# One group's transpose of q moved from TensorE to the crossbar DMA, ahead of the next batch's loads

## Chip, cores, metric

The kernel runs on one core of one Trainium2 chip. The metric is the device time of one execution in microseconds (us), lower is better; medians of several runs are given. Times of day inside a run ("at 49.2") are us from the start of the span of the profiled execution, which is about 2 us shorter than the device time.

## The reference, cut to what matters

Eight batches of linear attention feed one gated feed-forward block. In the attention, q is normalised along the head dimension and k along the sequence:

```python
q_s = softmax over d of q          # batch 8, heads 8, seq 576, head_dim 64
k_s = softmax over s of k
kv  = einsum('bhsd,bhse->bhde', k_s, v)
x   = einsum('bhsd,bhde->bhse', q_s, kv)          # -> 4608 tokens x 512
out = (silu(x @ w_gate) * (x @ w_val)) @ w_out    # d_ff 1536
```

## The kernel before

A batch is done in two groups of four heads; "(1,0)" below is batch 1, group 0. For each group three loads bring q, k and v (576 KB each). ScalarE takes exp of q and k, VectorE sums and scales q (`norm`, giving the tile `qs`), and q must then be transposed, because x = q·kv contracts over d. The kernel has two ways to do it. `tr` uses nine TensorE transposes into PSUM (the accumulator memory, of which the kernel uses eight banks) and two VectorE copies; `tr_dma` uses one transposing DMA (called the crossbar transpose here) on SyncE's queue:

```python
def tr(b, G, piece, eng):                 # nine 128x128 transposes in two pieces
    tp = psp.tile([128, 1024], BF16, tag="ps", name="tp")
    for t in range(t0, t1):
        nc.tensor.transpose(out=tp[:, ...], in_=s["qs"][:, t, :], identity=ident)
    copy(eng, s["qta"][:, :, t0:t1, :], tp[...])
# ... cut ...
def tr_dma(b, G):
    qt = at.tile([128, T, 2, 64], BF16, tag="qtd", name="qtd")
    nc.sync.dma_start_transpose(out=qt..., in_=s["qs"]...)
```

`kv_kn` makes kv on TensorE and its scaled copy kn (half on ScalarE, half on VectorE with `split`). `x` multiplies kn and the transposed q into `xp` and copies it to `xt`, the input of the feed-forward block. `m_unit` is one of twelve units of gate and value products with Silu; `o_unit` is one block of 128 tokens of the output product, with its copy and its two stores. The argument is about the hand-over from batch 0 to the chunk of batch 1's last 448 tokens:

```python
load(1, 0, "q", q, after=w_dma[-3]); load(1, 1, "q", q)
for G in range(NG): load(1, G, "k", k); load(1, G, "v", v)
load_group(2, 0)                       # q, k, v of (2,0)
for m in range(MT): m_unit(0, S, m)
exp(1, 0, "q"); exp(1, 1, "q"); exp(1, 0, "k")
cast_v(1, 0, nc.gpsimd); cast_v(1, 1, nc.gpsimd)
load_group(2, 1)
o_unit(0, nc.scalar); norm(1, 0)
o_unit(1, nc.scalar); exp(1, 1, "k"); norm(1, 1)
o_unit(2, nc.scalar)
for piece in BANKS: tr(1, 0, piece, nc.vector)
kv_kn(1, 0, split=True)
for piece in BANKS: tr(1, 1, piece, nc.vector)
exp(2, 0, "q")
def between():                         # in the middle of o_unit(3)
    kv_kn(1, 1, split=True); x_both(1, 0, nc.vector)
finish = o_unit(3, between=between)
exp(2, 0, "k"); x_both(1, 1); finish()
norm(2, 0); tr_dma(2, 0)
cast_v(2, 0, nc.gpsimd); cast_v(2, 1, nc.gpsimd)
exp(2, 1, "q"); exp(2, 1, "k")
# ... then the chunk: m_unit 0, 1, 2, kv_kn(2,0), m_unit 3, 4, x_both(2,0) ...
```

Each engine, and each queue of DMA issues, executes its own part of this list strictly in this order.

The softmax here doesn't subtract the row's maximum and nothing guards it: scores larger than these inputs give would overflow.

## Time and profile before

| | before |
|---|---|
| device time, median of 3 | 319.42 us (319.02 to 320.06) |
| TensorE busy (profile page) | 310.4 of 317.4 us |
| TensorE at batch 0's last output block | starts 49.24 |
| fourth unit of the chunk starts | 59.31 |

The first line is from the profile's page, the busy time of the engines (PE is TensorE, PEld its weight loads, DVE VectorE, ACT ScalarE, POOL GpSimd).

```profile
PE 310.4 (98%) x1920; PEld 157.1 (50%) x1948; DVE 175.5 (55%) x332; ACT 149.2 (47%) x224; POOL 31.1 (10%) x33
```

TensorE is the bottleneck: nothing that delays it is made good later. Next, TensorE's own timeline in the hand-over. The columns are start, duration, engine, source line, operation, tiles and count; a bracket at the end gives idle time before the piece and what ended it.

```profile
47.29 0.67 PE L160 MATMUL tp<-ident,qs 128*128 128x128 bf16 x9
47.89 0.70 PE L184 MATMUL kv<-vb,ek 64*128 64x129 bf16 x18
48.73 0.68 PE L160 MATMUL tp<-ident,qs 128*128 128x128 bf16 x9
49.24 1.46 PE L297 MATMUL o_ps<-wo,hr 128*128 128x512 bf16 x5
...
53.55 1.41 PE L270 MATMUL g_ps<-xt,wg 128*128 128x448 bf16 x4
54.80 0.92 PE L270 MATMUL u_ps<-xt,wv 128*128 128x448 bf16 x4
...
59.31 0.93 PE L270 MATMUL g_ps<-xt,wg 128*128 128x448 bf16 x4
...
311.02 2.81 PE L318 MATMUL o_ps<-wo,hr 128*128 128x256 bf16 x36
```

The first line is the work that the change removes. The second set of transposes, group 1's, starts at 48.73. VectorE finishes their input at 48.68 (the next two lines, from VectorE's timeline, are the scaling of q of groups 0 and 1; 47.31 + 1.36 is 48.67), so they could not start earlier whatever TensorE did before.

```profile
44.35 1.36 DVE L140 TENSOR_TENSOR qs<-eq,rr 128x1152 bf16<-128x1152 bf16 x1
...
47.31 1.36 DVE L140 TENSOR_TENSOR qs<-eq,rr 128x1152 bf16<-128x1152 bf16 x1
```

ScalarE's timeline shows the exps of batch 2 (eq, ek), the half of kn that ScalarE makes, the xt copies, the table load and the first Silu of the chunk (sg). None has a bracket that names a DMA: the loads are there in time. They land at 49.0, 50.5, 52.0, 53.6, 55.1 and 56.5 (issue plus the time to landing of each load), 1.5 us apart.

```profile
50.17 1.16 ACT L115 ACTIVATE eq<-q 128x1152 bf16<-128x1152 f32 x1
51.58 0.63 ACT L206 ACTIVATE kn<-kv,kvr 64x64 bf16<-64x64 f32 x2 [0.24 <-DVE kvr L196]
52.23 1.16 ACT L115 ACTIVATE ek<-k 128x1152 bf16<-128x1152 f32 x1
53.42 0.70 ACT L104 CAST xt<-xp 128x320 bf16<-128x320 f32 x2
54.01 1.18 ACT L115 ACTIVATE eq<-q 128x1152 bf16<-128x1152 f32 x1
55.14 1.16 ACT L115 ACTIVATE ek<-k 128x1152 bf16<-128x1152 f32 x1
56.32 1.28 ACT L278 ACT_TABLE_LOAD   x1
57.62 1.42 ACT L278 ACTIVATE sg<-g_ps 128x448 bf16<-128x448 f32 x3
```

The table of stages gives, for each stretch of 2 us, the busy time of each engine, and at the end the granted TensorE clock (1.00 is full), the DMA engines' share and GB/s. Before the change the DMA is full throughout.

```profile
45.00:47.00 2.00, 2.00 (x11) 0.90 (x10) 1.98 (x2) 1.57 (x3) 1.72 (x1) 1.00 1.05 391
47.00:49.00 2.00, 1.86 (x35) 1.38 (x33) 1.95 (x4) 0.81 (x2) 1.31 (x1) 1.00 1.05 388
49.00:51.00 2.00, 1.95 (x26) 1.10 (x26) 1.90 (x8) 1.45 (x3) 0.68 (x1) 1.00 1.06 395
```

### The profile page before, as it was taken

The numbers are of one execution on the slowest core, as the hardware profiler recorded it, in microseconds if no ns is written. First come the engines' busy times: TensorE is split into PE (matmuls) and PEld (weight loads), VectorE is DVE, ScalarE is ACT, GpSimd is POOL, SyncE is SP. The second block draws the span as 40 slices with busy tenths as digits, with TensorE's granted clock in tenths as the row PEclk, the third lists the DMA queues.
The fourth block names the chain that finished last, engine by engine and source line by source line (L and its number), as shares of the span: only waits on it lengthen the run. The fifth ranks groups of instructions, "written<-read, shape, count | busy, mean of one in ns | idle before, by whom it ended". The sixth has DMA issues, their size and how long they took to land.

```text
span 317.4 us, 5037 instructions
## 1 busy us (share of the span) xinstructions
PE 310.4 (98%) x1920; PEld 157.1 (50%) x1948; DVE 175.5 (55%) x332; ACT 149.2 (47%) x224; POOL 31.1 (10%) x33
## 2 busy tenths in 40 slices
PE   8999999999999999999999999999999999999995
PEld 6777744554445444444444444444444444444444
DVE  2934479964647664774577366746575333333422
ACT  4753387744763475547364547355734122312300
POOL 1930023121100110011001100020000000000000
PEclk9999999999999999999999999999999999999999
DMA  7999999449145905392519440963150213020134
GB/s 269 252 190 206 281 392 393 130 116 367 22 84 153 379 24 103 74 385 94 103 38 355 162 103 1 310 241 64 41 103 2 44 22 67 3 61 5 35 67 99
DMA packets 39176, 46.34 MB, mean 146 GB/s; under 512 B 16368, under 2 KB 22384, under 8 KB 39152
## 3 DMA queue, kind: packets, MB, share of 16 engines
q1 hardware_dynamic: 33104, 41.17, 42.5%
q0 software_dynamic: 5808, 4.72, 9.7%
q8 instruction: 15, 0.25, 0.3%
q10 hardware_dynamic: 240, 0.13, 0.2%
q14 instruction: 9, 0.07, 0.1%
HBM read 37.75 MB, written 9.44 MB: 149 GB/s over the span
## 4 chain that ended last, share of the span: by engine, by line
PE 82%; DMA 10%; DVE 3%; POOL 2%; ACT 1%; issue 1%; SPq 0%; DVEq 0%; ACTq 0%
PE g_ps L270 26%; PE o_ps L297 26%; PE u_ps L270 26%; DMA wo<-in_moe_w_out_dram 5%; PE kv L184 2%; DMA v<-in_v_dram 2%; DMA q<-in_q_dram 2%; PE xp L218 1%; POOL wg L92 1%; POOL wv L92 1%; DVE qs L140 1%; PE o_ps L318 1%; DVE rs L131 1%; DVE xt L226 0%; SPq L77 0%
## 5 line engine op out<-in xcount | busy, mean ns | idle before, releaser
L278 ACT ACTIVATE sg<-g_ps 128x512 bf16<-128x512 f32 (+2 forms) x120 | 64.9, 554 | 132.9 <-PE g_ps L270 126.8
L279 DVE TENSOR_TENSOR hr<-sg,u_ps 128x512 bf16<-128x512 bf16 (+2 forms) x120 | 74.9, 633 | 90.7 <-PE u_ps L270 84.1
L270 PE MATMUL g_ps<-xt,wg 128*128 128x512 bf16 (+2 forms) x469 | 110.3, 358 | 0.7
L270 PE MATMUL u_ps<-xt,wv 128*128 128x512 bf16 (+2 forms) x468 | 109.6, 357 | 0.7
L297 PE MATMUL o_ps<-wo,hr 128*128 128x512 bf16 x415 | 93.3, 379 | 0.3
L270 PEld LDWEIGHTS <-wv 128*128 128x128 bf16 x480 | 46.9, 98 | 46.9 <-issue 0.3
L270 PEld LDWEIGHTS <-wg 128*128 128x128 bf16 x480 | 45.3, 98 | 46.2 <-issue 2.6
L297 PEld LDWEIGHTS <-hr 128*128 128x128 bf16 x420 | 41.0, 98 | 49.1 <-issue 0.2
L106 POOL CAST vb<-v 128x1152 bf16<-128x1152 f32 x14 | 17.8, 1270 | 167.2 <-DMA v<-in_v_dram 115.0
L131 DVE TENSOR_REDUCE rs<-eq 128x18 f32<-128x1152 bf16 x16 | 21.6, 1352 | 21.9 <-ACT eq L115 21.8
L106 DVE COPY o_sb<-o_ps 128x512 f32<-128x512 f32 x32 | 21.1, 686 | 20.6 <-PE o_ps L297 20.6
L140 DVE TENSOR_TENSOR qs<-eq,rr 128x1152 bf16<-128x1152 bf16 x14 | 19.8, 1415 | 0.5
L115 ACT ACTIVATE eq<-q 128x1152 bf16<-128x1152 f32 x16 | 18.5, 1163 | 3.2 <-DMA q<-in_q_dram 3.1
L115 ACT ACTIVATE ek<-k 128x1152 bf16<-128x1152 f32 x16 | 18.4, 1152 | 1.3 <-DMA k<-in_k_dram 1.3
L278 ACT ACT_TABLE_LOAD x12 | 15.4, 1283 | 0.2
L208 DVE TENSOR_SCALAR kn<-kv,kvr 64x64 bf16<-64x64 f32 x52 | 14.7, 283 | 1.3
L115 ACT ACT_TABLE_LOAD x11 | 14.1, 1283 | 0.9 <-DMA q<-in_q_dram 0.7
L104 ACT CAST xt<-xp 128x320 bf16<-128x320 f32 (+1 forms) x30 | 10.5, 402 | 6.6 <-PE xp L218 6.6
L226 DVE CAST xt<-xp 128x320 bf16<-128x320 f32 (+1 forms) x32 | 13.1, 450 | 0.5 <-PE xp L218 0.5
L249 PE MATMUL warm_ps<-zero 128*128 128x256 bf16 x80 | 10.9, 302 | 1.1 <-DVE zero L338 1.1
L184 PE MATMUL kv<-vb,ek 64*128 64x129 bf16 x288 | 10.3, 218 | 0.2 <-DVE vb L106 0.2
L184 PEld LDWEIGHTS <-ek 64*128 64x128 bf16 x288 | 8.4, 94 | 3.9 <-ACT sg L278 2.1
(32 smaller groups left out, 64.5 us busy)
## 6 DMA issues: line engine op xcount, KB each, us to landing
q<-in_q_dram SPq DMA_DIRECT2D x16, 576.0 KB, 7.0
k<-in_k_dram SPq DMA_DIRECT2D x16, 576.0 KB, 8.5
v<-in_v_dram SPq DMA_DIRECT2D x16, 576.0 KB, 9.4
out_dram<-o_sb SPq DMA_DIRECT2D x70, 128.0 KB, 2.4
wo<-in_moe_w_out_dram POOLq DMA_DIRECT2D x3, 512.0 KB, 19.0
wg<-in_moe_w_gate_dram POOLq DMA_DIRECT2D x2, 512.0 KB, 11.3
wv<-in_moe_w_val_dram POOLq DMA_DIRECT2D x2, 512.0 KB, 13.1
wg<-in_moe_w_gate_dram POOLq DMA_DIRECT2D x2, 256.0 KB, 6.0
```

The source lines that it names most:

```text
L106: eng.tensor_copy(out=out, in_=in_)
L115: nc.scalar.activation(out=s["e" + what], in_=raw[what, b, G].rearrange("p h (t d) -> p t h d", d=64), func=AF.Exp,)
L131: nc.vector.reduce_sum(out=rs, in_=s["eq"].rearrange("p t h d -> p (t h) d"), axis=mybir.AxisListType.X)
L140: eng.tensor_mul(s["qs"].rearrange("p t (h d) -> p (t h) d", d=64), s["eq"].rearrange("p t h d -> p (t h) d"), s["rr"].to_broadcast([128, ...
L184: nc.tensor.matmul(out=s["kv"][g][:, 0:129], lhsT=s["ek"][r, t, :, :].rearrange("p h d -> p (h d)"), rhs=s["vb"][r, t, 0:129], start=(t == 0),
L208: nc.vector.tensor_scalar_mul(out_, src, sc)
L226: nc.vector.tensor_copy(out=xt[:, 2 * G + 1, c0:c0 + n], in_=xp[1][:, 0:n])
L249: nc.tensor.matmul(out=ps[:, 0:256], lhsT=zero[:, 0:128], rhs=zero, start=True, stop=True)
L270: nc.tensor.matmul(out=p_[:, 0:w_], lhsT=w[:, kk, ms], rhs=xt[:, kk, c:c + w_], start=(kk == 0), stop=(kk == KT - 1),)
L278: nc.scalar.activation(out=sg[:, 0:w_], in_=g_ps[:, 0:w_], func=AF.Silu)
L279: nc.vector.tensor_mul(hr[:, m, r:r + w_], sg[:, 0:w_], u_ps[:, 0:w_])
L297: nc.tensor.matmul(out=o_ps, lhsT=hr[:, m, r0:r0 + 128], rhs=wo[:, m, :], start=(m == 0), stop=(m == MT - 1),)
```

## The change

The intent is to take nine transposes and two copies off TensorE and VectorE and let the DMA do them. The loads of batch 2 are moved behind the transpose in SyncE's order, so that the transpose does not have to queue behind 3.5 MB of loads.

```diff
@@ after batch 1's loads
             load(1, G, "v", v)
-        load_group(2, 0)
 
         for m in range(MT):
@@ hand-over
         cast_v(1, 1, nc.gpsimd)
-        load_group(2, 1)
         o_unit(0, nc.scalar)
         norm(1, 0)
+        tr_dma(1, 0)
+        load_group(2, 0)
+        load_group(2, 1)
         o_unit(1, nc.scalar)
         exp(1, 1, "k")
         norm(1, 1)
         o_unit(2, nc.scalar)
-        for piece in BANKS:
-            tr(1, 0, piece, nc.vector)
         kv_kn(1, 0, split=True)
```

## The prediction

> **What bounds the kernel.** TensorE: busy 310.4 of 317.4 us, clock granted in full (page). From 54.6 us on, the chain of waits is almost only TensorE, so a delay made by this change is paid to the end. The change lies in the hand-over from batch 0's products to the next chunk (39 to 60 us). There the DMA is full: 381 to 404 GB/s from 37 to 55 us (stage table).
>
> **Removed.** Nine transposes of (batch 1, group 0) on TensorE (0.68 us in the timeline, starting 47.3) and two VectorE copies of qt (0.82 us, 48.6). Neither is in the chain of waits: TensorE's next transposes, group 1's, start at 48.73 and wait for VectorE's qs of group 1, which ends at 48.68 whatever TensorE does. With group 0's gone, TensorE does kv at 47.4, then waits about 0.7 us for the same qs. Expected gain: 0 to 0.4 us.
>
> **Added.** One crossbar transpose on the SyncE queue. Other such transposes here take 1.3 us to issue and 3.2 us to land. It waits for qs of group 0 (45.7) and for the first output stores ahead of it on SyncE (about 45.2 to 46.4), so I put its issue at 46.4 and its landing at 49.7 to 50.5. Its reader, xp of group 0, runs at 51.3, so should not wait. (The Trainium skill, "Advanced Engine Details and Errata", X-Bar Transpose, says trn2 transposes are as fast as regular DMAs; here 295 KB (128x1152 bf16) take 3.2 us, while loads stream at about 390 GB/s; I use the trace.)
>
> **Moved.** All six loads of batch 2 (576 KB each, 1.5 us apart when streaming). Before, queued behind batch 1's, they land at 49.0, 50.5, 52.0, 53.6, 55.1, 56.5; the exps on ScalarE never wait. Afterwards they are issued only from 47.7, behind the transpose. The same sequence, transpose then six loads, stands twice in the trace (66.5 and 97.5): from the transpose's issue the loads land at about +5.5, +7.1, +8.9 to 9.8, +10.4 to 11.3, +12.3 to 12.8, +14. So q, k of group 0 land at about 51.9 and 53.5, q, k of group 1 at 57 and 58.9.
>
> **Critical path.** ScalarE runs in order: exp q (2,0), kn of group 1, exp k (2,0), xt copies, exp q, k (2,1), table load, first Silu. Late q pushes kn and xt: the chunk's start slips from 54.6 by about 1 us. Late k (2,1) puts the first Silu at 58.9 + 1.15 + 1.28 = 61.3 instead of 57.6. TensorE can run three units and kv ahead with eight banks; the fourth unit then needs the bank that the first Silu frees: 61.9 instead of 59.4. So about 2.5 us lost in all (not the sum), less a few tenths gained.
>
> **Prediction: 321.7 us**, 319.6 to 323.6 in 8 of 10. Faster by over 2%: 0.01; within 2%: 0.96; slower by over 2%: 0.03.
>
> **What shows it.** TensorE idles after kv of (1,0), group 1's transposes still start near 48.7; ScalarE shows waits for DMA q and k of batch 2 between 50 and 60 us (before: none); DMA rate dips at 45 to 49 us; first Silu of the second chunk at about 61 us; a TensorE wait for Silu near the fourth unit; from 65 us on the timelines run 2 to 3 us apart.
>
> **What would make it wrong.** Loads landing sooner after an earlier transpose issue (then 0 to 1 us lost, or slightly faster); xp waiting for a transpose that lands late (more lost); later transfers, shifted by 2 us, missing their readers.

## The result, and the profile after

The changed kernel takes 321.96 us (median of 6 runs, 321.31 to 322.98) against 319.35 us for the kernel before in the same rounds. The ratio is 1.0084 (95% interval 1.0061 to 1.0108), within 2%. Ratios are computed as the mean time of one kernel's runs over that of the other's of the same rounds, so they are not quite the ratio of the medians quoted. Executions over 1.5% slower than the fastest of the same kernel are left out of the means.

TensorE's timeline of the changed kernel, to be held against the one of before:

```profile
47.31 0.70 PE L184 MATMUL kv<-vb,ek 64*128 64x129 bf16 x18
48.30 0.68 PE L160 MATMUL tp<-ident,qs 128*128 128x128 bf16 x9 [0.29 <-DVE qs L140]
48.81 1.46 PE L297 MATMUL o_ps<-wo,hr 128*128 128x512 bf16 x6
50.20 0.70 PE L184 MATMUL kv<-vb,ek 64*128 64x129 bf16 x18
50.83 0.44 PE L218 MATMUL xp<-qtd,kn 64*64 64x320 bf16 x8
51.20 1.47 PE L297 MATMUL o_ps<-wo,hr 128*128 128x512 bf16 x6
52.60 0.32 PE L218 MATMUL xp<-qt,kn 64*64 64x320 bf16 x1
54.15 0.44 PE L218 MATMUL xp<-qt,kn 64*64 64x320 bf16 x7 [1.23 <-ACT kn L206]
54.52 0.55 PE L270 MATMUL g_ps<-xt,wg 128*128 128x448 bf16 x2
56.07 0.90 PE L270 MATMUL g_ps<-xt,wg 128*128 128x448 bf16 x2 [1.00 <-ACT xt L104]
...
62.46 0.93 PE L270 MATMUL g_ps<-xt,wg 128*128 128x448 bf16 x4
```

Group 0's transposes are gone and TensorE waits for qs of group 1 instead. VectorE finished it 0.43 us earlier in this trace (48.24), and the output block starts 0.43 us earlier, 48.81 against 49.24: the removal gained nothing there. xp of group 0 (50.83) reads the crossbar's result without a wait; the transpose was issued at 46.02 and landed 3.4 us later. Then come two waits that before did not have, 1.23 us for kn and 1.00 us for xt, both ScalarE's. SyncE's issues and ScalarE's timeline say why:

```profile
44.74 1.18 SPq L289 DMA_DIRECT2D out_dram<-o_sb  x2
46.02 1.41 SPq L172 DMA_TRANSPOSE qtd<-qs  x1
47.49 0.57 SPq L77 DMA_DIRECT2D q<-in_q_dram  x1
```

```profile
52.27 1.17 ACT L115 ACTIVATE eq<-q 128x1152 bf16<-128x1152 f32 x1 [3.29 <-DMA q<-in_q_dram]
53.46 0.64 ACT L206 ACTIVATE kn<-kv,kvr 64x64 bf16<-64x64 f32 x2
54.12 1.17 ACT L115 ACTIVATE ek<-k 128x1152 bf16<-128x1152 f32 x1
55.31 0.70 ACT L104 CAST xt<-xp 128x320 bf16<-128x320 f32 x2
56.69 1.17 ACT L115 ACTIVATE eq<-q 128x1152 bf16<-128x1152 f32 x1 [0.68 <-DMA q<-in_q_dram]
58.25 1.17 ACT L115 ACTIVATE ek<-k 128x1152 bf16<-128x1152 f32 x1 [0.39 <-DMA k<-in_k_dram]
59.43 1.28 ACT L278 ACT_TABLE_LOAD   x1
60.73 1.42 ACT L278 ACTIVATE sg<-g_ps 128x448 bf16<-128x448 f32 x3
```

ScalarE stands 3.29 us before exp of q (2,0), because that load was issued only at 47.49 and landed at 52.2. ScalarE takes its work in order, so kn and xt, which need nothing of batch 2, stand behind it. The loads of q, k of (2,0) and q, k of (2,1) land at 52.2, 53.6, 56.6 and 58.1 (issue plus time to landing; predicted 51.9, 53.5, 57 and 58.9), and the first Silu starts at 60.73 instead of 57.62. In the table of stages the DMA rate falls where before it was full (the run with the loads moved and no transpose has the same dip, 226, 184 and 373 GB/s, so the dip alone does not point to the transpose), and TensorE's clock falls a little later:

```profile
45.00:47.00 2.00, 2.00 (x12) 0.88 (x9) 1.93 (x4) 1.57 (x2) 1.29 (x1) 1.00 0.83 238
47.00:49.00 2.00, 1.71 (x30) 1.14 (x29) 1.93 (x5) 1.21 (x3) 1.61 (x1) 1.00 1.14 188
49.00:51.00 2.00, 2.00 (x32) 1.06 (x30) 0.90 (x4) 0.00 (x0) 0.24 (x1) 1.00 0.81 243
...
53.00:55.00 2.00, 0.85 (x9) 0.35 (x9) 0.84 (x4) 1.94 (x4) 0.00 (x0) 1.00 1.05 411
55.00:57.00 2.00, 1.00 (x4) 0.40 (x3) 1.97 (x4) 1.30 (x4) 1.15 (x1) 0.69 1.07 391
57.00:59.00 2.00, 2.00 (x6) 0.73 (x5) 1.93 (x3) 1.61 (x2) 0.00 (x0) 0.50 1.02 372
```

The granted clock of 0.50 near 57 to 59 was not in the prediction. It is there in two of the six runs by their mean clock (0.992 and 0.995, both 322.95 to 322.98 us); the four others have 1.000 and 321.31 to 322.12 us. The profile above is one of the two. The repeat below was profiled at full clock, and there the chunk's third and fourth matmul and its fourth unit read:

```profile
55.67 0.54 PE L270 MATMUL g_ps<-xt,wg 128*128 128x448 bf16 x2 [0.99 <-ACT xt L104]
56.04 0.92 PE L270 MATMUL u_ps<-xt,wv 128*128 128x448 bf16 x4
...
60.97 0.92 PE L270 MATMUL g_ps<-xt,wg 128*128 128x448 bf16 x4 [0.35 <-ACT sg L278]
...
312.67 2.81 PE L318 MATMUL o_ps<-wo,hr 128*128 128x256 bf16 x36
```

At full clock the fourth unit waits 0.35 us for the PSUM bank that the first Silu frees. At the halved clock TensorE was itself too slow to run into that wait: from the third matmul to the following kv it took 5.77 us (56.07 to 61.84) instead of 4.25 (55.67 to 59.92).

Not all of the loss lies in the hand-over. From the start of batch 0's output product (39.52 before, 39.59 in the repeat) to the last output block (311.02 and 312.67, the last lines of the two timelines) the repeat takes 1.6 us longer; I call this the long stretch below. From there to the end of the span it takes 6.80 us where before it is 6.35. This 0.4 us at the very end stands in every kernel here that has one more DMA than before (6.78 to 6.80 us; 6.72 in the one with two more) and in none that has not (6.35 in the runs with the loads moved and with the removal alone). SyncE's list of waits for the last stores shows 1.3 us in one wait instead of 0.7 us in three. That would fit a fixed order of closing waits in which one more DMA moves the last store to an earlier place, but no run tested this.

### The profile page after: what moved, and what is told of

Its sections match the earlier page's. It is cut to its first block, busy times and chain, and to the rows that moved or that the text cites. A ratio compares the mean times of both kernels' runs of the same rounds, so it can differ in the third digit from the quotient of the medians.

```text
span 321.0 us, 5045 instructions
## 1 busy us (share of the span) xinstructions
PE 312.8 (97%) x1939; PEld 157.1 (49%) x1939; DVE 174.7 (54%) x330; ACT 149.7 (47%) x224; POOL 30.8 (10%) x33
## 2 busy tenths in 40 slices
DMA packets 40360, 46.63 MB, mean 145 GB/s; under 512 B 17552, under 2 KB 23568, under 8 KB 40336
## 4 chain that ended last, share of the span: by engine, by line
PE 81%; DMA 11%; POOL 2%; ACT 2%; DVE 2%; SPq 1%; issue 0%; ACTq 0%; DVEq 0%
PE g_ps L270 26%; PE u_ps L270 26%; PE o_ps L297 25%; DMA wo<-in_moe_w_out_dram 5%; DMA q<-in_q_dram 4%; DMA v<-in_v_dram 2%; PE kv L184 2%; PE xp L218 1%; POOL wg L92 1%; POOL wv L92 1%; PE o_ps L318 1%; DVE rs L131 1%; ACT eq L115 1%; SPq L77 0%; DVE qs L140 0%; ACT L115 0%
## 5 line engine op out<-in xcount | busy, mean ns | idle before, releaser
L270 PE MATMUL g_ps<-xt,wg 128*128 128x512 bf16 (+2 forms) x480 | 112.3, 360 | 1.0 <-ACT xt L104 1.0
L270 PE MATMUL u_ps<-xt,wv 128*128 128x512 bf16 (+2 forms) x480 | 111.8, 360 | 0.0
L226 DVE CAST xt<-xp 128x320 bf16<-128x320 f32 (+1 forms) x32 | 13.1, 449 | 1.6 <-PE xp L218 1.6
```

What stands on the lines that cost most here:

```text
L226: nc.vector.tensor_copy(out=xt[:, 2 * G + 1, c0:c0 + n], in_=xp[1][:, 0:n])
L270: nc.tensor.matmul(out=p_[:, 0:w_], lhsT=w[:, kk, ms], rhs=xt[:, kk, c:c + w_], start=(kk == 0), stop=(kk == KT - 1),)
```

## The experiments

My theory: the loss is the lateness of the six loads, through ScalarE's order; it is made mostly by the transpose that goes ahead of them, and the removed TensorE work was not in the chain of waits. Rivals: the move of the loads alone costs it; the transposed q arrives late; the reduced clock is the loss; and, for the removal, that nine transposes are worth their 0.6 us once nothing else is disturbed.

All kernels were correct except one. Its output is wrong, which doesn't matter for the time. Time is given with that of the kernel before in the same rounds.

### Loads moved, no crossbar transpose

```diff
 (against the changed kernel)
-        tr_dma(1, 0)
...
         o_unit(2, nc.scalar)
+        for piece in BANKS:
+            tr(1, 0, piece, nc.vector)
```

> The loads of batch 2 stand where the change puts them (after the first output stores), but there is no crossbar transpose: group 0 of batch 1 is transposed on TensorE as before. Theory A (the transpose ahead of the loads is what delays them: 1.4 us of issue on SyncE and some 1.7 us of DMA time, the mere move past the first stores is nearly free because batch 1's loads keep the DMA busy until then): first load issued about 46 instead of 47.5, q of (2,0) lands about 49 to 49.7, k of (2,1) about 55.5 to 56, time within 0.5 us of before (319.4 to 319.9). Rival B (the move of the loads is itself the cost): q (2,0) lands near 52, time about 321.5. The clock stays at 1.00 under A.

Measured: 319.97 us against 319.39, ratio 1.0013 (0.9999 to 1.0026). The first load is issued at 46.77, and the exps wait little:

```profile
50.98 1.16 ACT L115 ACTIVATE eq<-q 128x1152 bf16<-128x1152 f32 x1 [0.47 <-DMA q<-in_q_dram]
```

So the move alone costs about 0.4 us in the mean (the interval just touches zero; the long stretch of its trace is 0.4 us longer), and the larger part of the loss, some 2 us, comes with the transpose ahead of the loads, 0.4 us of it at the end of the kernel. The detail was off: q of (2,0) landed just before 51, not by 49.7, and k of (2,1) at 56.9, not by 56. The loads are late by about as much from the move as from the transpose, but the first delay is swallowed, because before q lay ready 1.2 us before it was read (49.0 and 50.17). What is left is a wait of 0.33 us in the fourth unit for the first Silu's bank.

### Crossbar transpose, loads left ahead of it

```diff
 (against the kernel before)
         norm(1, 0)
+        tr_dma(1, 0)
         o_unit(1, nc.scalar)
...
-        for piece in BANKS:
-            tr(1, 0, piece, nc.vector)
```

> The crossbar transpose is put in, but all loads of batch 2 stay where they were, ahead of it on the SyncE queue. If the queue serves its transfers in order, the transpose lands only after the last load (56.5 in before), at about 57 to 60 us instead of 50.9, and xp of group 0, ready at 51.3, waits some 6 to 8 us for it: 325 to 328 us, slower than the change. If transfers of one queue pass each other freely, the transpose lands about 3 to 5 us after its issue and the time is near before's 319.4.

Measured: 328.79 us against 319.39, ratio 1.0284 (1.0267 to 1.0300). The transpose was issued at 49.45 and landed 9.1 us later; xp of group 0 waited 7.27 us for it. This is the only reason why the loads have to move: behind them the transpose is late for its reader. Part of the late issue is the program's own: in the compiled order the transpose also waits for the DMA issued eight before it, here q of (2,0) (0.9 us in SyncE's list of waits). In this run and the next two the loss is more than the wait of xp: TensorE, idle for 6.7 to 8.1 us, was granted half its clock in this stage (0.50 in the tables of stages), and the mean clock is 0.983 to 0.989 in every one of their runs.

### The transpose on ScalarE's queue

```diff
 (against the kernel before)
-        nc.sync.dma_start_transpose(
+        eng.dma_start_transpose(
...
-        load_group(2, 1)
         o_unit(0, nc.scalar)
         norm(1, 0)
+        tr_dma(1, 0, nc.scalar)
+        load_group(2, 1)
...
-        for piece in BANKS:
-            tr(1, 0, piece, nc.vector)
```

> The crossbar transpose is issued from ScalarE's queue at about 45.8, group 0's loads of batch 2 stay where they were, group 1's are issued right behind. The loads land within 1 us of before, so the first Silu starts within 1 us of before's 57.6. My theory: TensorE's saved 0.7 us is not in the chain of waits, because its next work waits for VectorE's qs of group 1; so time equals before within 0.5 us (319.0 to 320.2), no gain. Rival (the nine transposes are worth their 0.6 us once the loads are not disturbed): 318.6 to 318.8. If the transpose shares the 16 engines badly with the loads and lands after 51.3, xp waits and the time rises by as much.

Measured: 328.08 us against 319.39, ratio 1.0271 (1.0255 to 1.0287). The main expectation was wrong, and the side condition named last came true far beyond what I thought. The transpose was issued at 45.56, as planned, and landed 12.1 us later, at 57.7, when only the last of the loads was still to land (58.1). TensorE's list of waits in this stage:

```profile
PE xp L218 <- DMA qtd<-qs: 6.7, 1, 6.7
```

(columns: total us, times, longest). A queue of its own does not give the transpose a lane of its own. The Trainium skill, "DMA: Bandwidth & Descriptors", section "Queues, rings and completion order", says that each DMA engine serves one queue in ring order and takes turns between its queues packet by packet; the page of the changed kernel counts 1,184 more packets under 512 B than that of before (17,552 less 16,368), so one transpose is some 74 small packets for each of 16 engines, while the loads' packets are larger. That it gets one small turn for each large one would fit, but no run here measured the turns; what is shown is the 12.1 us.

### Both groups' transposes on ScalarE's queue

```diff
 (against the run before this one)
         o_unit(2, nc.scalar)
-        kv_kn(1, 0, split=True)
-        for piece in BANKS:
-            tr(1, 1, piece, nc.vector)
+        tr_dma(1, 1, nc.scalar)
+        kv_kn(1, 0)
```

> As the run with the transpose on ScalarE's queue, and group 1's transposes go the same way, so that TensorE no longer waits for qs of group 1 before batch 0's last product block. My theory says that only then a gain is there: that block starts at about 48.1 instead of 49.2, and xp of group 1, at 53.0 before, can start at about 52 if its transpose, issued at about 48.7 to 50, has landed by then: 318.3 to 319.2 us. If the second transpose, beside the loads, takes over 4 us to land, xp of group 1 waits for it and the time is 319.5 to 321.

Measured: 328.94 us, ratio 1.0298 (1.0281 to 1.0314): a miss for the same cause. The output block does start earlier (48.43), as the theory said, but xp of group 0 waits 8.13 us for the first transpose, which takes 13.1 us to land (the second 12.2). Whether the earlier start pays could not be seen here; the edit also leaves out the split of kn of (1,0), so it is not a pure test of it.

### The changed kernel once more

No edit.

> The changed kernel itself, once more, as the baseline of this chip and to see how its runs divide. In its six runs so far two had a mean granted clock of 0.992 to 0.995 and 322.95 us, four had 1.000 and 321.3 to 322.1. Expected: the same two groups, about 1.0 to 1.2 us apart, because TensorE, nearly idle for 3.5 us (52.6 to 56.1), is sometimes granted half its clock for about 3 us afterwards.

Measured: 322.31 us (321.54 to 323.58) against 319.40, ratio 1.0099 (1.0078 to 1.0120). Three of six runs lie at 321.5 to 321.7, three at 322.9 to 323.6. Of those three only one has a reduced mean clock (0.995); two have 1.000. So the two groups are real, but the clock does not explain all of the slower one.

### Filler on TensorE while it waits

```diff
 (against the changed kernel)
         finish = o_unit(3, between=between)
+        warm_up(12)
         exp(2, 0, "k")
         x_both(1, 1)
+        warm_up(14)
         finish()
```

> The changed kernel with 22 matmuls of zeros (about 0.11 us each) put on TensorE where it waits for kn and xt of group 1. They compute nothing that is used. If the reduced clock follows from TensorE's idle time, every run has the mean clock 1.000 and the slow group of about 323 us is gone: 321.3 to 322.0 in all runs; the first matmuls of the chunk may start 0.1 to 0.3 us later. If the clock has another cause, the groups stay.

Measured: 322.03 us (321.61 to 325.53), ratio 1.0098 (1.0066 to 1.0130). (The kernel ran 26 filler matmuls, not 22 as announced.) Five of six runs lie at 321.6 to 322.5 and none has a clock under 0.997, which fits the clock theory; but with two runs of six, then one of six, showing the reduced clock without filler, six runs prove little. The sixth run, the profiled one, is the slowest of all with 325.53 us at full clock: there the loads of (2,1) landed late (exp of its k waited until 61.89), for a reason that the trace does not show, and TensorE was already 1.3 us late before the hand-over (batch 0's output product starts at 40.80 instead of 39.52). Inconclusive, and the mean is no better: TensorE's idle time is filled, not shortened.

### One load ahead of the transpose, the v's last

```diff
 (against the changed kernel)
             load(1, G, "v", v)
+        load(2, 0, "q", q)
...
         tr_dma(1, 0)
-        load_group(2, 0)
-        load_group(2, 1)
+        load(2, 0, "k", k)
+        load(2, 1, "q", q)
+        load(2, 1, "k", k)
+        load(2, 0, "v", v)
+        load(2, 1, "v", v)
```

> The changed kernel with one load, q of (2,0), ahead of the transpose (where it was before the change), and behind the transpose the two k's and q of (2,1) ahead of the v's. If the whole loss is the late q and k, it goes: q (2,0) lands near 49 and exp does not wait; the transpose lands near 51.2, about when xp needs it; k (2,0) near 52.7, so xt is not late and the chunk starts within 0.4 us of before; k (2,1) near 55.7, so the first Silu ends before the fourth unit needs its bank. Time 319.2 to 320.2 us, as before the change and not faster, since TensorE still waits for qs of group 1. If another cost of the transpose is at work, the time stays above 321.

Measured: 320.56 us (319.82 to 320.78) against 319.40, ratio 1.0028 (1.0015 to 1.0041); the median is 0.4 us above the range that I gave. The transpose took 4.7 us to land behind that load, and xp still did not wait. exp of q (2,0) ran at 49.14 without a wait, and the chunk's third matmul had 0.49 us to wait for xt. About 70% of the loss is gone (the ratio falls from 1.0099 to 1.0028) though the transpose, its place before the other five loads and its issue time are all still there. There is a new small wait, 0.25 us of kv (2,0) for the cast of v, which now lands late, but it is not the rest of the loss: in the profiled run (319.87 us) the long stretch takes 271.47 us, as before (271.50), and what is left is the 0.4 us at the end. Three of the five runs are slower, at 320.6 to 320.8 us; none of them was profiled, and why stays open. The edit does two things, one load ahead and the v's last, and no run separates them.

### ScalarE's order changed alone

```diff
 (against the changed kernel)
-        exp(2, 0, "q")
...
-        exp(2, 0, "k")
         x_both(1, 1)
+        exp(2, 0, "q")
+        exp(2, 0, "k")
         finish()
```

> The changed kernel with ScalarE's order changed alone: kn and the xt copies of group 1 go ahead of both exps of (2,0), so that late loads no longer delay the start of the chunk. My reading is that two waits end close together, the late start (1.9 us) and the late first Silu (about 2.3 us), and the longer counts, not the sum. Then the chunk starts about 1.9 us earlier, on time, but its fourth unit waits about 2.3 us for the bank of the first Silu, which stays at 60.7, and the time changes by only 0 to 0.5 us: 321.0 to 321.9. If the late start were the loss and the Silu did not bind, the time would fall to about 319.6.

Measured: 321.77 us (321.35 to 323.75), ratio 1.0080 (1.0060 to 1.0100), as expected. The chunk starts on time and the wait moves to the bank of the first Silu:

```profile
53.42 1.41 PE L270 MATMUL g_ps<-xt,wg 128*128 128x448 bf16 x4
...
61.26 0.92 PE L270 MATMUL g_ps<-xt,wg 128*128 128x448 bf16 x4 [2.02 <-ACT sg L278]
```

Two waits ended within half a microsecond of each other. Taking one away shows the other; the loss was the longer of the two, not the sum. (The ratio is 0.2% below that of the changed kernel in the same rounds, and the two intervals overlap.)

### The removal alone (wrong)

```diff
 (against the kernel before)
+        zq = const.tile([128, 2, T, 64], BF16, name="zq", tag="zq")
+        nc.gpsimd.memset(zq, 0.0)
...
-        for piece in BANKS:
-            tr(1, 0, piece, nc.vector)
+        st[1, 0]["qt"] = [zq[:, g, :, :] for g in range(2)]
```

> The kernel before with only the removal: group 0's nine TensorE transposes and the two VectorE copies are left out, nothing takes their place, and xp of batch 1, group 0, reads a tile of zeros (the result is wrong on purpose). No load moves and there is no crossbar transpose. My theory: the removed work is not in the chain of waits, because group 1's transposes wait for VectorE's qs anyway; the time stays at before's 319.4 within 0.3 us (319.0 to 319.6), and TensorE shows an idle time or a longer wait of 0.5 to 0.7 us before group 1's transposes. Rival: the nine transposes are worth their 0.6 us and more: 318.4 to 318.9.

Measured: 319.16 us against 319.65, ratio 0.9988 (0.9974 to 1.0002). That is 0.4 us in the mean, at the top of the predicted 0 to 0.4, below the 0.6 us and more of the rival, and not clear of zero. In the profiled run the long stretch is 0.2 us shorter than before. TensorE shows the wait that the transposes used to fill:

```profile
49.02 0.68 PE L160 MATMUL tp<-ident,qs 128*128 128x128 bf16 x9 [0.46 <-DVE qs L140]
```

### A try at the better version

```diff
 (against the run with one load ahead)
-        for piece in BANKS:
-            tr(1, 1, piece, nc.vector)
...
         def between():
+            for piece in BANKS:
+                tr(1, 1, piece, nc.vector)
             kv_kn(1, 1, split=True)
-            x_both(1, 0, nc.vector)
...
-        exp(2, 0, "k")
+        x_both(1, 0)
         x_both(1, 1)
+        exp(2, 0, "k")
...
-                steps = {2: lambda: kv_kn(2, 0, True), 4: lambda: x_both(2, 0),
+                steps = {3: lambda: kv_kn(2, 0, True), 5: lambda: x_both(2, 0),
```

> A try at a version that beats both: q of (2,0) ahead of the transpose, the two k's and q of (2,1) ahead of the v's; TensorE does the first half of batch 0's last product block before group 1's transposes, so that it no longer waits for qs of group 1; xp of both groups after the second half; kv of (2,0) one unit later, so that it does not wait for the late v. By the durations seen, the block starts at about 48.1 instead of 48.7 to 49.2 and the chunk 0.2 to 0.6 us earlier, with the first Silu near 58.9 just in time. Expected 318.8 to 319.8 us; if the late loads still cost something, up to 320.3. If it is not under 319.4, the transposes' time on TensorE is not to be had by this route.

Measured: 319.42 us (319.16 to 319.62) against 319.65, ratio 0.9993 (0.9980 to 1.0006). With the crossbar transpose kept, the whole loss is gone and TensorE no longer waits for qs (the output block starts at 48.36, right behind kv). In time no version here beats the kernel before. But the trace shows why it is a draw: the long stretch takes 270.86 us, 0.64 us less than before, which is about what nine transposes take, and the end of the kernel takes 0.44 us more (6.79 instead of 6.35); the run also reached the stretch 0.3 us later, within what runs differ by. It would fit that the removed work pays once TensorE has other work ready, and that the end takes most of it back; but this run also changes the order on TensorE, the same order with the transposes kept was not run, and it is one profiled run of each kernel, so this is not shown.

## Why the prediction was right

- **Removed work is worth 0 to 0.4 us.** Right. Nothing at the output block in the changed kernel; 0.4 us in the mean, interval touching zero, with the removal alone.
- **The transpose does not make its reader wait.** Right: it landed at 49.4 (46.02 and 3.4 us; predicted 49.7 to 50.5), and xp read it at 50.83.
- **Late loads.** Right to within 1 us for each of the four that matter, because the trace of before already held the same sequence, a transpose with six loads behind it, twice. The prediction put all of their lateness on one place, "behind the transpose"; the run with the loads moved but no transpose shows two parts, the move past the first stores and the transpose itself. The first alone nearly fits ScalarE's slack (0.4 us lost); with the second it does not.
- **The late start of the chunk and the late first Silu, the longer one counting.** Right in kind: with the late start removed, the time fell by only about 0.2% and the Silu's bank took over with 2.02 us. In size the late start was taken too small. It was to be "about 1 us"; at full clock it is 1.2 us, taken at the first value product of the chunk (u_ps, 56.04 against 54.80), or 1.5 when it is counted from the output block's start. The first Silu started at 60.38 and 60.73 instead of 61.3, because k of (2,1) landed 0.7 to 1.1 us sooner than predicted. So its bank added only 0.35 us at full clock where the prediction had it add about 1.5, and the fourth unit is 1.7 us late (60.97 against 59.31), not 2.5.
- **The end of the kernel.** Not predicted, and not a matter of the hand-over: 0.4 us.
- **The clock.** Not predicted. In some runs TensorE was granted half its clock for about 3.4 us after its waits (0.88, 0.50, 0.50, 0.50 and 0.92 in the slices of 1 us from 55 to 60). In the profiled one TensorE took 1.5 us longer for the first three units; by my estimate 1.1 us of it counts, since the first Silu (0.54 us from 60.73) would have held the fourth unit until about 61.3, and it started at 62.46. The Trainium skill, "TensorE: Matmul & The Clock Gate", section "What's actually happening", says that the clock is halved after an idle window of about 3.4 us and that this window runs free of the program, so that where it falls varies. The trace agrees with the half (0.50) and with the variation (two of six runs, then one of six). It does not show an idle window of that length: from 53 us until the clock fell in the slice from 55 to 56 us TensorE worked 0.9 of 3 us, and its longest idle time was 1.23 us. That the waits bring the clock down is therefore likely, not shown, and the slower runs at full clock remain unexplained.

The total, 321.7 predicted and 321.96 measured, is closer than its parts deserve, and that is partly luck. The path of the loss was right, but at full clock the hand-over lost 1.6 us in the trace where the prediction had 2.5 less a few tenths. What made up for it were the 0.4 us at the end of the kernel and, in two of the six runs, the reduced clock; the four runs at full clock have a median of 321.7 us, the profiled repeat 321.54.

## What to carry to other kernels

Moving work to an idle engine pays only if the old engine has other work ready at that moment; look at what its next instruction waits for. Compare the stretch that was changed, and not only the total: here 0.4 us of the total came from the end of the kernel, far from the edit. An operation put ahead of loads in an in-order DMA queue delays all of them, and an engine that runs in order passes the delay on to work that needs none of those loads: read the slack of each load (when it lands, when it is first read) before moving it. When two waits end close together, count the longer one, and expect the second to appear when the first is removed.

## What the Trainium skill lacked or had wrong

- "Advanced Engine Details and Errata", section "X-Bar Transpose (TRN2)", says that transposes are as fast as regular DMAs. Here a 295 KB transpose (128x1152 bf16) took 3.2 us from issue to landing in most cases, and 3.3 to 5.7 us on SyncE's queue with other transfers about (9.1 behind all six loads); an output store of 128 KB took 2.4 us, and the quickest load of 576 KB 3.5 us (issued at 0.7 us in the trace of before). These are times for single transfers of different sizes; the rate of a transpose was not measured, so no run here decides whether the sentence holds.
- "DMA: Bandwidth & Descriptors", section "Issuing engines are not separate DMA queues", says that DMAs of different issuing engines interleave. It lacks what this means for a transpose beside streaming loads: 12.1 to 13.1 us to landing from ScalarE's queue, against 3.4 us ahead of the loads on SyncE's.
- "VectorE: DVE Perf Modes", section "The three transpose paths", gives 390 ns for one 128x128 bf16 transpose on TensorE and 1309 ns by the crossbar. Nine in a row took 0.67 us on TensorE, that is 75 ns each, and 3.2 us by the crossbar, 0.36 us each; the figures for one alone mislead for a batch.
